# One PSUM tile per bank group in an attention-and-feed-forward kernel: three tiles in place of one of four banks

## The chip, the cores and the metric

The kernel runs on one core of a Trainium2 chip. The metric is the device time of one execution in microseconds (us), the median of three runs. Names of engines: PE is the TensorE matmul engine, ACT the ScalarE, DVE the VectorE, POOL the GpSimd, SP the queue that issues most transfers.

## What is computed

```python
def _attn_ref(q, k, v, agents):
    scale = 1.0 / np.sqrt(q.shape[-1])
    def sm(a, b):
        s = scale * (a @ b.transpose(0, 2, 1))
        s = s - s.max(-1, keepdims=True)
        e = np.exp(s)
        return e / (e.sum(-1, keepdims=True) + 1e-09)
    a2k = sm(agents, k)
    agent_v = a2k @ v
    q2a = sm(q, agents)
    return q2a @ agent_v
def _moe_ref(x, w_in, w_out):
    h = np.maximum(x @ w_in, 0.0)
    return h * h @ w_out
```

q, k and v are 4 x 12480 x 128, there are 49 agents per batch element, and the feed-forward part takes the 49920 rows of the attention's output through 2048 hidden channels (w_in 128 x 2048, w_out 2048 x 128).

## The kernel before

The agents' table is folded into the first feed-forward weight: `agent_v @ w_in` gives a table of 49 x 2048 per batch element, held as a high part (`aw_hi`) and a rest (`aw_ex`), so that the hidden layer comes straight from the query softmax, whose turned weights are `w` (98 rows and 30 copied rows) and `x` (the rest of the rows, copied to four row groups by transfers). Hidden channels are worked on in chunks of 128 for `G` = 480 tokens. Two groups of four chunks make a **session** (`m` == 2; four sessions at the start and two at the end have one group only, `m` == 1). There are 205 full sessions, and four of them make one block `g` of 960 tokens.

All eight PSUM banks belong to two sets of four banks, the tiles `A` and `B`. Sessions swap them. In a session whose first tile is, say, `A`:

- `first` (line 384) writes the first four chunks to the four banks of A: four matmuls of `w` with `aw_hi`, four of `x` with `aw_ex`. Then it does the same for the other four chunks in B.
- `rectified` (line 408) takes the ReLU out of PSUM into the SBUF tile `r` on ACT: for A first bank 0 alone, then banks 1 to 3; later B in one instruction of four banks.
- `second` (line 423) multiplies the squared hidden values of the session two before (`LAG` = 2) with `w_out`: 24 matmuls that all add up in `o`, which is **bank 0 of A**. The first four take `g_lo` of the first half, then sixteen alternate `wo_lo` and `wo_hi` with `g_hi`, and the last four take `g_lo` of the second half. After `LEAD` = 6 of them the phase "P" comes, in which PE does the side work, and then the other 18.
- The side work is the query softmax of a later block (`queries`, line 311) and the keys and values of the next batch element (`background`, line 448). It writes the other banks of A: bank 1 for query scores (`ASKED`), bank 2 for everything of `background` (`BLOCKS`), bank 3 for the turned query weights (`TURNED`).
- ACT then squares `r` in place (phase "A1" lies ahead of it, "A3" behind the session). DVE rounds the squares of the session before to `g_hi`, takes the rests `g_lo` in two halves with the side work of phase "D" between them, and at last adds `o` to `ob` in SBUF (`copied_out`, line 437). Every second session ends with a transfer of `ob` to HBM.

ACT, DVE and PE work through lists in the order in which the code issues them (`queued`, line 60, and `Ordered`, line 69, chain each instruction to the one before on its engine). Waits between engines are set by the framework from tiles: an instruction that writes a tile waits for those that read or wrote that tile before. The lines that matter for this:

```python
    ASKED, BLOCKS, TURNED = 1, 2, 3
    ...
        x = sets.tile([P, SET, 512], F32, name=tags[0])
        other = lambda: sets.tile([P, SET, 512], F32, name=tags[1])
    ...
        o = desk["at"][:, s % LAG if s < len(EARLY) else 0, :G]
    ...
            if m == 2:
                rectified(r, x, 0, 1)
                rectified(r, x, 1, 3)
```

Of the kernel before, what the change touches and what calls it, by code (L numbers as in the profile page):

```python
# [9 lines left out]
F32 = mybir.dt.float32  # L10
F32R = mybir.dt.float32r
U32 = mybir.dt.uint32
AF = mybir.ActivationFunctionType
# [4 lines left out]
P = 128  # L18
# [4 lines left out]
G = BLK // 2  # L23
SET = 4
EARLY = (1, 1, 1, 1)
SIZES = (2, 2)
LATE = (2, 1, 1)
LAG = 2
# [13 lines left out]
def agent_attention_relu2(ctx: ExitStack, tc: tile.TileContext, qT, kT, v, agT, w_in, w_out, outT):  # L42
    nc = tc.nc
    C, NTOK = qT.shape
    _, B, NA = agT.shape
# [14 lines left out]
    def queued(issue, eng, *args, **kw):  # L60

        with tc.issue_after(chain[eng]) if eng in chain else ExitStack():
            ins = issue(*args, **kw)  # L63
        chain[eng] = ins.ins
        return ins
# [3 lines left out]
    class Ordered:  # L69
        def __init__(self, eng, always=False):  # L70
            self.eng, self.always = eng, always
# [7 lines left out]
    pe, act, dve = (Ordered(e, True) for e in (nc.tensor, nc.scalar, nc.vector))  # L79
# [18 lines left out]
    ones = const.tile([P, P], F32, name="ones")  # L98
# [58 lines left out]
        pool.tensor_add(lo, t, rest)  # L157

    desk = {}
    ASKED, BLOCKS, TURNED = 1, 2, 3  # L160

    def bank():
        if alone[0]:
            return ps_h.tile([P, 2, 512], F32, name="h")[:, 0, :]
        return desk["at"][:, BLOCKS, :]

    def query_bank(slot):
        if alone[0]:
            return ps_a.tile([P, 512], F32, name="psa")
        return desk["at"][:, slot, :]  # L170

# [193 lines left out]
    def products(k, outs):  # L367
        g, j, at = place(k)
        b = g // NB
        w, x = weights[g][j]  # L370

        def main(n, **kw):
            cs = slice((at + n) * P, (at + n + 1) * P)
            queued(nc.tensor.matmul, nc.tensor, outs[n], state[b]["hi"][:, cs], w, **kw)

        def extra(n, **kw):
            t = (at + n) % NQ
            rows = slice(t * 32, t * 32 + NL)
            lo = state[b]["lo"][rows, (at + n) // NQ, :]
            queued(nc.tensor.matmul, nc.tensor, outs[n], lo, x[rows, :], **kw)  # L380

        return main, extra

    def first(k, m, x, other):
        outs = [x[:, n, :G] for n in range(SET)]
        main, extra = products(k, outs)
        for n in range(SET):
            main(n, start=True, stop=False)
        with tc.high_priority():
            for n in range(SET):  # L390
                extra(n, start=False, stop=True)
        if m == 2:
            y = other()
            outs += [y[:, n, :G] for n in range(SET)]
            with tc.high_priority():
                for n in range(SET, 2 * SET):
                    extra(n, start=True, stop=False)
            for n in range(SET, 2 * SET):
                main(n, start=False, stop=True)
            return x, y  # L400
        return x, None

    def held(name, dtype, m, at):
        if m == 2 or at == 0:
            tiles[name] = ffn.tile([P, 2 * SET, G], dtype, name=name, bufs=2)
        return tiles[name] if m == 2 else tiles[name][:, at : at + SET, :]

    def rectified(r, x, at, n):
        queued(nc.scalar.activation, nc.scalar, r[:, at : at + n, :], x[:, at % SET : at % SET + n, :G], AF.Relu)

    def squared(r, at, n):
        queued(nc.scalar.activation, nc.scalar, r[:, at : at + n, :], r[:, at : at + n, :], AF.Square)
# [35 lines left out]
    def background(b):  # L448
        kt = load_keys(b, 0, kv, "kt")
        for i in range(NK):  # L450
            yield "P", 1, True
            nxt = load_keys(b, i + 1, kv, "kt") if i + 1 < NK else load_values(b, 0, kv, "vt")
            yield from scores(b, i, kt)
            kt = nxt
        yield from maxima(b)
        vt = kt
        for i in range(NK):
            nxt = load_values(b, i + 1, kv, "vt") if i + 1 < NK else None
            yield from values(b, i, vt)
            vt = nxt  # L460
        yield from whole_sums(b)
        yield from tables(b)
# [3 lines left out]
    def step(gen):  # L466

        with ExitStack() as es:
            for ins in behind:
                es.enter_context(tc.issue_after(ins))  # L470
            return next(gen, None)
# [24 lines left out]

    def table(n, pieces=1):
        near = aw.tile([P, 512], F32R, name="aw_lo", bufs=3)
        pws = [bank() for _ in range(pieces)] if n < 2 else [desk["at"][:, n - 1, :]]
        w = 512 // pieces  # L500
        for x, pw in enumerate(pws):
            pe.matmul(pw[:, :w], turn["avT"], win[:, n * 512 + x * w : n * 512 + (x + 1) * w], start=True, stop=True)
        for x, pw in enumerate(pws):
            part = near[:, x * w : (x + 1) * w]
            act.activation(part, pw[:, :w], AF.Copy, scale=turn["signs"][:, :1])
            dve.scalar_tensor_tensor(
                out=hi[:, n * 512 + x * w : n * 512 + (x + 1) * w], in0=pw[:, :w], scalar=turn["signs"][:, 1:],
                in1=part.bitcast(F32), op0=ALU.mult, op1=ALU.subtract,
            )
# [13 lines left out]
    with tc.tile_pool(name="pre", bufs=PRE) as pre, tc.tile_pool(name="dec", bufs=2) as dec:  # L523
# [56 lines left out]
        for i in range(NK):  # L580
            _, rows, nt = blocks[i]
            n = rows * nt // 2
# [5 lines left out]
            s = sp.tile([P, 512], F32, name="s")[:, :n]  # L588
# [8 lines left out]
            if i in (0, 4, 8):  # L597
                at = i // 4 * WIDE
# [13 lines left out]
        f = small.tile([P, 1], F32, name="f")  # L612
# [88 lines left out]
    sets = ctx.enter_context(tc.tile_pool(name="sets", bufs=1, space=PSUM))  # L701
    ffn = ctx.enter_context(tc.tile_pool(name="ffn", bufs=4))

    sessions, starts, at = [], [], 0
# [47 lines left out]
    made, x, early = {}, None, None  # L752
    todo["end"] = starts[NB]
    for s in range(len(sessions) + LAG):
        k, m = sessions[s] if s < len(sessions) else (total, 0)
        if s == LAG:
            behind = [chain[eng] for eng in (nc.tensor, nc.sync, nc.scalar, nc.vector, nc.gpsimd)]
        if s in starts and s // 2 and starts.index(s) % NB == 0:
            assert not todo["next"]
            b = starts.index(s) // NB  # L760
            if b + 1 < B:
                todo.update(gen=background(b + 1), done=0, start=s, end=starts[(b + 1) * NB])
                todo["next"] = (*step(todo["gen"]), s)
        phase("L", s)

        tags = "AB" if s <= len(EARLY) or (s - len(EARLY)) % 2 == 0 else "BA"
        x = sets.tile([P, SET, 512], F32, name=tags[0])
        other = lambda: sets.tile([P, SET, 512], F32, name=tags[1])
        if s == 0:
            early = other()  # L770
        desk["at"] = early if s < len(EARLY) else x
        o = desk["at"][:, s % LAG if s < len(EARLY) else 0, :G]

        if m:
            x, y = first(k, m, x, other)
            r = held("r", F32, m, place(k)[2] % (2 * SET))
            made[s] = r
            if m == 2:
                rectified(r, x, 0, 1)
                rectified(r, x, 1, 3)  # L780
            else:
                for n in (0, 2):
                    rectified(r, x, n, 2)
        if s < LAG:
            alone[0] = True
            if s:
                for _ in range(5):
                    pe.matmul(desk["at"][:, 0, :P], ones, ones, start=True, stop=True)
            table(s + 2)
            alone[0] = False  # L790
        work = second(*sessions[s - LAG], o) if s >= LAG else iter(())
        for _ in range(LEAD):
            next(work, None)
        phase("P", s)
        if m == 2:
            rectified(r, y, SET, SET)
        phase("A1", s)
        if m == 2:
            squared(r, 0, 2 * SET)
        elif m:  # L800
            for n in (0, 2):
                squared(r, n, 2)
        if 1 <= s <= len(sessions):
            z, n = sessions[s - 1]
            old = made.pop(s - 1)
            hi = held("g_hi", F32R, n, place(z)[2] % (2 * SET))
            los = [ffn.tile([P, SET, G], F32R, name="g_lo", bufs=3) for _ in range(n)]
            parts[z] = hi, los
            if n == 2:
                rounded(hi, old, 0, 2 * SET)  # L810
                rest(los[0], old, hi, 0, SET)
                phase("D", s)
                rest(los[1], old, hi, SET, SET)
            else:
                for i in (0, 2):
                    rounded(hi, old, i, 2)
                    rest(los[0], old, hi, i, 2)
                phase("D", s)
        run(work)
        if s >= LAG:  # L820
            copied_out(*sessions[s - LAG], o)
        phase("A3", s)
# [35 lines left out]
```

## Time and profile before

| what | value |
|---|---|
| median of three runs | 2305.52 us (2304.36 to 2311.49) |
| profiled execution | 2305.71 us, its span 2303.9 us |
| mean granted TensorE clock | 0.987 of full speed |
| PE busy | 1954.8 us, 85% of the span |
| DVE busy | 1727.2 us, 75% |
| ACT busy | 1600.2 us, 69% |
| transfers | 57 GB/s mean, 17.1% of the 16 engines' time |

A timeline row gives the start in us, the length in us, the engine, the instruction as output<-inputs, how many rows of one kind it merges, and in brackets the idle time of the engine just before it with what ended that. Matmuls are pipelined: the next one starts before the printed length of the one before is over. All rows carry line 63, the helper that issues them, so the tile names tell the places apart. The first 84 us prepare the first batch element and the weights; the sessions run from there to about 2300 us.

### The profile page before, as it was taken

The numbers are of one execution on the slowest core, as the hardware profiler recorded it, in microseconds if no ns is written. First come the engines' busy times: TensorE is split into PE (matmuls) and PEld (weight loads), VectorE is DVE, ScalarE is ACT, GpSimd is POOL, SyncE is SP. The second block draws the span as 40 slices with busy tenths as digits, with TensorE's granted clock in tenths as the row PEclk, the third lists the DMA queues.
The fourth block names the chain that finished last, engine by engine and source line by source line (L and its number), as shares of the span: only waits on it lengthen the run. The fifth ranks groups of instructions, "written<-read, shape, count | busy, mean of one in ns | idle before, by whom it ended". The sixth has DMA issues, their size and how long they took to land.

```text
span 2303.9 us, 39309 instructions
## 1 busy us (share of the span) xinstructions
PE 1954.8 (85%) x17186; PEld 1466.7 (64%) x17186; DVE 1727.2 (75%) x1487; ACT 1600.2 (69%) x1213; POOL 20.8 (1%) x24
## 2 busy tenths in 40 slices
PE   8788888887888888888888888888888888888888
PEld 5566666665666666666666666666656666666666
DVE  7777777876777777787677777778777777777776
ACT  5766767766666767677576667777667777777775
POOL 3000000000000000000000000000000000000000
PEclk9999999999999999999899999999999999999999
DMA  9212112211112112111012210211111111101100
GB/s 335 80 57 75 53 47 75 65 54 42 34 63 69 56 49 70 63 60 60 30 34 73 68 48 30 78 59 56 43 31 33 41 33 41 33 32 36 32 24 20
DMA packets 54816, 131.44 MB, mean 57 GB/s; under 512 B 6508, under 2 KB 34828, under 8 KB 54644
## 3 DMA queue, kind: packets, MB, share of 16 engines
q1 hardware_dynamic: 54644, 128.93, 17.1%
q8 instruction: 135, 2.21, 0.4%
q14 instruction: 37, 0.30, 0.0%
HBM read 80.97 MB, written 25.56 MB: 46 GB/s over the span
## 4 chain that ended last, share of the span: by engine, by line
PE 72%; ACT 20%; DVE 6%; issue 2%; DVEq 0%; POOL 0%; ACTq 0%; POOLq 0%
PE A L63 36%; PE B L63 35%; ACT r L63 16%; ACT w L63 3%; DVE m L63 1%; ACT s L63 1%; DVE e L63 1%; DVE g_lo L63 1%; DVE g_hi L63 1%; DVE mx L63 0%; DVE t L63 0%; DVE aw_lo L63 0%; DVE av L63 0%; PE h L63 0%; ACT aw_hi L63 0%
## 5 line engine op out<-in xcount | busy, mean ns | idle before, releaser
L63 DVE TENSOR_TENSOR g_lo<-r,g_hi 128x1920 fp32r<-128x1920 f32 (+1 forms) x422 | 894.5, 2126 | 7.7 <-PE B L63 0.2
L63 ACT ACTIVATE r<-r 128x3840 f32<-128x3840 f32 (+1 forms) x217 | 712.1, 3285 | 2.2
L63 ACT ACTIVATE r<-B 128x1920 f32<-128x1920 f32 (+2 forms) x309 | 372.9, 1242 | 332.1 <-PE B L63 332.1
L63 ACT ACTIVATE r<-A 128x1920 f32<-128x1920 f32 (+3 forms) x318 | 380.1, 1232 | 225.4 <-PE A L63 225.4
L63 DVE CAST g_hi<-r 128x3840 fp32r<-128x3840 f32 (+1 forms) x217 | 448.4, 2066 | 0.1
L63 PE MATMUL A<-g_hi,wo_lo 128*128 128x480 f32 x832 | 333.3, 401 | 105.4 <-DVE e L63 44.0
L63 PE MATMUL B<-g_hi,wo_lo 128*128 128x480 f32 x832 | 331.3, 398 | 81.1 <-ACT w L63 46.0
L63 PE MATMUL A<-g_hi,wo_hi 128*128 128x480 f32 x832 | 324.7, 390 | 0.0
L63 PE MATMUL B<-g_hi,wo_hi 128*128 128x480 f32 x832 | 319.6, 384 | 0.0
L63 PE MATMUL A<-g_lo,wo_hi 128*128 128x480 f32 x832 | 228.0, 396 | 76.0 <-ACT r L63 76.0
L63 PE MATMUL B<-g_lo,wo_hi 128*128 128x480 f32 x832 | 227.8, 396 | 67.8 <-ACT r L63 67.8
L63 PEld LDWEIGHTS A<-g_hi,wo_lo 128*128 128x128 f32 x832 | 161.4, 194 | 147.7 <-issue 47.6
L63 PEld LDWEIGHTS A<-g_lo,wo_hi 128*128 128x128 f32 x832 | 149.8, 190 | 137.1 <-ACT r L63 117.6
L63 PEld LDWEIGHTS B<-g_hi,wo_lo 128*128 128x128 f32 x832 | 158.5, 191 | 121.1 <-ACT w L63 55.8
L63 PEld LDWEIGHTS B<-g_lo,wo_hi 128*128 128x128 f32 x832 | 149.6, 189 | 128.5 <-ACT r L63 109.1
L63 PE MATMUL A<-w,aw_hi 128*128 128x480 f32 x840 | 228.1, 393 | 2.6 <-DVE aw_hi L63 1.6
L63 DVE TENSOR_TENSOR ob<-B,ob 128x480 f32<-128x480 f32 x105 | 69.0, 657 | 211.6 <-PE B L63 211.6
L63 PE MATMUL B<-w,aw_hi 128*128 128x480 f32 x824 | 224.4, 394 | 0.0
L63 DVE COPY ob<-A 128x480 f32<-128x480 f32 x103 | 67.7, 657 | 196.7 <-PE A L63 190.7
L63 PEld LDWEIGHTS A<-w,aw_hi 128*128 128x128 f32 x840 | 150.0, 188 | 58.1 <-issue 34.2
L63 PEld LDWEIGHTS B<-w,aw_hi 128*128 128x128 f32 x824 | 147.3, 189 | 53.7 <-issue 34.4
L63 PEld LDWEIGHTS A<-g_hi,wo_hi 128*128 128x128 f32 x832 | 161.6, 194 | 24.3
(169 smaller groups left out, 1355.5 us busy)
## 6 DMA issues: line engine op xcount, KB each, us to landing
qt<-in_qT SPq DMA_DIRECT2D x52, 480.0 KB
out_T<-ob SPq DMA_DIRECT2D x104, 240.0 KB
kt<-in_kT SPq DMA_DIRECT2D x36, 512.0 KB
vt<-in_v SPq DMA_DIRECT2D x36, 512.0 KB
x<-w SPq DMA_DIRECT2D x416, 35.6 KB
ahead<-in_kT SPq DMA_DIRECT2D x12, 512.0 KB
ahead<-in_v SPq DMA_DIRECT2D x12, 512.0 KB
w<-w SPq DMA_DIRECT2D x104, 56.2 KB
```

The lines of the kernel that those rows point to most:

```text
L63: ins = issue(*args, **kw)
```

## The change

Each set of four banks becomes three tiles: one bank (`A0`), one bank (`A1`), and a pair (`A2`). `o` lies in the first, the work of `background` moves to the second (slot 1), and the query work keeps to the pair (slots 2 and 3). The ReLU takes one instruction per tile, so three of 480, 480 and 960 columns in place of two (480 and 1440) for the first half of a session and of one (1920) for the second half, and of two (960 each) in sessions of one group.

```diff
-    ASKED, BLOCKS, TURNED = 1, 2, 3
+    BLOCKS, ASKED, TURNED = 1, 2, 3
+    GROUPS = ((0, 1), (1, 1), (2, 2))
+
+    class Banks:
+        def __init__(self, tag):
+            self.tiles = [sets.tile([P, n, 512], F32, name=f"{tag}{at}") for at, n in GROUPS]
+
+        def __getitem__(self, n):
+            x = min(n, len(GROUPS) - 1)
+            return self.tiles[x][:, n - GROUPS[x][0], :]
...
-        return desk["at"][:, BLOCKS, :]
+        return desk["at"][BLOCKS]
...
-        return desk["at"][:, slot, :]
+        return desk["at"][slot]
...
-        outs = [x[:, n, :G] for n in range(SET)]
+        outs = [x[n][:, :G] for n in range(SET)]
...
-    def rectified(r, x, at, n):
-        queued(nc.scalar.activation, nc.scalar, r[:, at : at + n, :], x[:, at % SET : at % SET + n, :G], AF.Relu)
+    def rectified(r, x, at):
+        for bank, (n, m) in zip(x.tiles, GROUPS):
+            queued(nc.scalar.activation, nc.scalar, r[:, at + n : at + n + m, :], bank[:, :, :G], AF.Relu)
...
-        x = sets.tile([P, SET, 512], F32, name=tags[0])
-        other = lambda: sets.tile([P, SET, 512], F32, name=tags[1])
+        x = Banks(tags[0])
+        other = lambda: Banks(tags[1])
...
-        o = desk["at"][:, s % LAG if s < len(EARLY) else 0, :G]
+        o = desk["at"][s % LAG if s < len(EARLY) else 0][:, :G]
...
-            if m == 2:
-                rectified(r, x, 0, 1)
-                rectified(r, x, 1, 3)
-            else:
-                for n in (0, 2):
-                    rectified(r, x, n, 2)
+            rectified(r, x, 0)
...
-            rectified(r, y, SET, SET)
+            rectified(r, y, SET)
```

PE and DVE keep their instructions in the same order. What differs on PE is what its instructions wait for. The next two listings are one session with side work for a query block, on PE: from the second half of `first` (into A) over the start of `second` (`g_lo`, `g_hi` into B) to the turned query weights (`identr`) and what follows them. Before:

```order
L63 MATMUL A<-x_8966,aw_ex 128x480 x3
L63 MATMUL A<-w_8965,aw_hi 128x480 x4
L63 MATMUL B<-g_lo,wo_hi 128x480 [waits Activation_49]
L63 MATMUL B<-g_lo,wo_hi 128x480 x3
L63 MATMUL B<-g_hi,wo_lo 128x480
L63 MATMUL B<-g_hi,wo_hi 128x480
L63 MATMUL B<-identr,pp 98x120 x4
L63 MATMUL B<-g_hi,wo_lo 128x480 [waits Activation_49]
```

After, the same session, where the number behind a name is the tile's own (9941 is the bank with `o`, 9943 the pair of banks of the same set):

```order
L63 MATMUL A_9954<-x_9582,aw_ex 128x480 x2
L63 MATMUL A_9952<-w_9581,aw_hi 128x480
L63 MATMUL A_9953<-w_9581,aw_hi 128x480
L63 MATMUL A_9954<-w_9581,aw_hi 128x480 x2
L63 MATMUL B_9941<-g_lo,wo_hi 128x480 [waits Activation_49]
L63 MATMUL B_9941<-g_lo,wo_hi 128x480 x3
L63 MATMUL B_9941<-g_hi,wo_lo 128x480
L63 MATMUL B_9941<-g_hi,wo_hi 128x480
L63 MATMUL B_9943<-identr,pp 98x120 [waits Activation_49]
L63 MATMUL B_9943<-identr,pp 98x120 x3
L63 MATMUL B_9941<-g_hi,wo_lo 128x480
```

The wait on ACT behind the four `identr` matmuls is gone, and one ahead of them has come. The wait of the first `g_lo` stands, now for the tile of one bank.

On ACT the ReLUs of one session and the start of the next, with the ReLU of a first half at the top. Before:

```order
L63 ACTIVATE r<-A 128x480
L63 ACTIVATE r<-A 128x1440
L63 ACTIVATE r<-B 128x1920
L63 COPY s<-A 128x392
L63 ACTIVATE r<-r 128x3840
```

After:

```order
L63 ACTIVATE r<-A_11475 128x480
L63 ACTIVATE r<-A_11476 128x480
L63 ACTIVATE r<-A_11477 128x960
L63 ACTIVATE r<-B_11486 128x480
L63 ACTIVATE r<-B_11487 128x480
L63 ACTIVATE r<-B_11488 128x960
L63 COPY s<-A_11476 128x392
L63 ACTIVATE r<-r 128x3840
```

Three instructions have become six, with the same columns and the same neighbours.

On the SP queue some loads of keys and values stand behind the five small transfers of the query weights (`w`, `x`) that they stood ahead of. Before:

```order
L314 DMA qt<-in_qT 128x960
L180 DMA kt<-in_kT 128x1024 x2
L350 DMA w_1882<-w_1882 30x480
L352 DMA x_1883<-w_1882 19x480 x4
L446 DMA out_T<-ob 128x480
```

After:

```order
L323 DMA qt<-in_qT 128x960
L189 DMA kt<-in_kT 128x1024
L359 DMA w_1966<-w_1966 30x480
L361 DMA x_1967<-w_1966 19x480 x4
L189 DMA kt<-in_kT 128x1024
L456 DMA out_T<-ob 128x480
```

The second load of keys has moved behind `x`.

## Rows read from the trace of the kernel before

**Rows 1.** The page, part 1: busy us, share of the span, instructions of each engine.

```profile
PE 1954.8 (85%) x17186; PEld 1466.7 (64%) x17186; DVE 1727.2 (75%) x1487; ACT 1600.2 (69%) x1213; POOL 20.8 (1%) x24
```

**Rows 2.** Who waited for whom, PE: us in total, times, longest us.

```profile
PE A L63 <- ACT r L63: 77.0, 104, 1.9
PE B L63 <- ACT r L63: 68.5, 103, 1.9
PE B L63 <- ACT w L63: 46.0, 71, 0.7
...
PE A L63 <- DVE mb L63: 0.9, 2, 0.5
```

**Rows 3.** Groups of instructions by form: count, busy us, mean ns, idle before, releasers.

```profile
L63 PE MATMUL A<-g_hi,wo_lo 128*128 128x480 f32 x832 | 333.3, 401 | 105.4 <-DVE e L63 44.0 <-DVE av L63 28.4 <-DVE aw_lo L63 21.0
...
L63 PE MATMUL B<-g_hi,wo_lo 128*128 128x480 f32 x832 | 331.3, 398 | 81.1 <-ACT w L63 46.0 <-ACT s L63 14.4 <-DVE av L63 8.3
```

**Rows 4.** Timeline of PE, one session without side work and the next one's start.

```profile
590.22 1.03 PE L63 MATMUL A<-w,aw_hi 128*128 128x480 f32 x4
...
591.82 1.14 PE L63 MATMUL B<-w,aw_hi 128*128 128x480 f32 x4
593.68 1.13 PE L63 MATMUL A<-g_lo,wo_hi 128*128 128x480 f32 x4 [0.72 <-ACT r L63]
594.65 0.38 PE L63 MATMUL A<-g_hi,wo_lo 128*128 128x480 f32 x1
...
598.14 1.04 PE L63 MATMUL A<-g_lo,wo_hi 128*128 128x480 f32 x4
599.02 1.03 PE L63 MATMUL B<-w,aw_hi 128*128 128x480 f32 x4
...
600.30 0.39 PE L63 MATMUL A<-x,aw_ex 19*128 19x480 f32 x4
```

**Rows 5.** Timeline of PE around the turned query weights.

```profile
603.82 0.48 PE L63 MATMUL B<-identr,pp 120*98 120x120 f32 x4
604.95 0.49 PE L63 MATMUL B<-g_hi,wo_lo 128*128 128x480 f32 x1 [0.65 <-ACT w L63]
605.27 0.38 PE L63 MATMUL B<-g_hi,wo_hi 128*128 128x480 f32 x1
```

**Rows 6.** Timeline of PE around query scores.

```profile
613.96 0.89 PE L63 MATMUL A<-ag,qt 128*32 128x49 f32 x64
616.21 0.49 PE L63 MATMUL A<-g_hi,wo_lo 128*128 128x480 f32 x1 [1.36 <-DVE e L63]
```

**Rows 7.** Timeline of PE, query scores followed at once by other side work.

```profile
1003.48 0.89 PE L63 MATMUL A<-ag,qt 128*32 128x49 f32 x64
1004.20 0.89 PE L63 MATMUL A<-d,vt 128*32 128x49 f32 x64
```

**Rows 8.** Groups by form on ACT, the ReLUs.

```profile
L63 ACT ACTIVATE r<-B 128x1920 f32<-128x1920 f32 x103 | 183.7, 1784 | 0.0
...
L63 ACT ACTIVATE r<-A 128x1440 f32<-128x1440 f32 x103 | 140.8, 1367 | 0.0
...
L63 ACT ACTIVATE r<-A 128x480 f32<-128x480 f32 x103 | 59.1, 574 | 216.0 <-PE A L63 216.0
```

**Rows 9.** Timeline of ACT, the two ReLUs of a first half merged.

```profile
600.53 1.83 ACT L63 ACTIVATE r<-B 128x480 f32<-128x480 f32 x2 [1.78 <-PE B L63]
```

**Rows 10.** Timeline of DVE, the sum's copy at a session's end.

```profile
599.28 0.66 DVE L63 COPY ob<-A 128x480 f32<-128x480 f32 x1 [1.40 <-ACT r L63]
```

**Rows 11.** Stages: us; PE, PEld, DVE, ACT, POOL busy; PE clock, DMA share, GB/s.

```profile
84.00:2276.00 2192.00, 1866.99 (x16520) 1407.52 (x16519) 1651.88 (x1369) 1543.61 (x1114) 0.00 (x0) 0.99 0.16 50
...
399.36:410.44 11.08, 9.51 (x109) 7.36 (x108) 9.52 (x12) 8.21 (x7) 0.00 (x0) 1.00 0.18 56
...
1100.00:1170.00 70.00, 58.26 (x322) 42.64 (x321) 48.74 (x39) 45.05 (x33) 0.00 (x0) 0.93 0.10 31
```

**Rows 12.** Timeline of SP, two loads of keys merged.

```profile
177.30 12.37 SPq L180 DMA_DIRECT2D kt<-in_kT  x2
```

More of the change, by code (lines that the diff above doesn't have):

```diff
@@ L393, in first @@
             y = other()
-            outs += [y[:, n, :G] for n in range(SET)]
+            outs += [y[n][:, :G] for n in range(SET)]
             with tc.high_priority():
@@ L498, in table @@
         near = aw.tile([P, 512], F32R, name="aw_lo", bufs=3)
-        pws = [bank() for _ in range(pieces)] if n < 2 else [desk["at"][:, n - 1, :]]
+        pws = [bank() for _ in range(pieces)] if n < 2 else [desk["at"][4 - n]]
         w = 512 // pieces
@@ L787, in agent_attention_relu2 @@
                 for _ in range(5):
-                    pe.matmul(desk["at"][:, 0, :P], ones, ones, start=True, stop=True)
+                    pe.matmul(desk["at"][0][:, :P], ones, ones, start=True, stop=True)
             table(s + 2)
```

## The prediction

> **What bounds the kernel now.** I read the busy times first: PE is at 85%, DVE at 75%, ACT at 69% [rows 1]. PE is the fullest engine, yet it stands still for about 350 us of the span, so the next view is who it waits for. Two kinds of wait make up nearly all of it. The first matmul of `second` waits for ACT's ReLU in 207 sessions, 77.0 + 68.5 us [rows 2]. The first `g_hi` matmul behind side work waits for whoever reads that side work: DVE's `e`, `av` and `aw_lo`, ACT's `w` and `s`; its two groups sum to 105.4 + 81.1 = 186.5 us [rows 3], in about 184 waits, the first and the last kind of which stand in [rows 2] (46.0 us in 71 for `w`, 0.9 us in 2 for `mb`). In both kinds the matmul writes bank 0 (`o`), and the engine that it waits for is reading another bank of the same tile. For the first kind the timeline says so by length: in a session without side work the wait ends at 593.68 [rows 4], and the two merged ReLUs of a first half take 1.83 us [rows 9], of which the bank-0 one is 0.57 [rows 8]; PE waits for the second one too, which it does not need. So these waits come from where the tiles are cut, and the order of the work on PE would allow the next matmul.
>
> **Change, term 1: the ReLU wait.** A0 now holds `o` alone, and its ReLU lasts 0.57 us [rows 8] from when the first half's sums are in, while PE still has the second half's eight matmuls to issue (600.30 to some 601.5 in [rows 4]). So that ReLU ends before PE comes to `g_lo`, and I take the wait as gone. What a session gains is read as start to start, since a stopped pipeline drains and fills again: four matmuls in a row take 0.88 us (598.14 to 599.02), so `g_lo` could start at 591.82 + 0.88 = 592.70 and starts at 593.68, 0.98 later; and its own four then take 0.97 us (593.68 to 594.65) in place of 0.88 [rows 4]. That is 1.07 us a session, against 0.72 of printed idle. 207 x 1.07 = **221 us**.
>
> **Term 2: the side-work waits.** All 186.5 us of idle time [rows 3] go, because bank 1 and the pair are other tiles than `o`. The next write to them is the other half of the next session, many us later. Drain and fill add to it: behind `identr` PE restarts 1.13 us after its start, where the four need at most 0.48, so 0.65 plus a first matmul that takes 0.32 in place of 0.22, 0.75 in all for 0.65 of idle [rows 5]; behind query scores the gap is 2.25 us [rows 6], the same work followed at once by other work takes 0.72 [rows 7], so 1.53 for 1.36 of idle, plus 0.10. I take 0.18 over the idle time for each of 184: 33 us. Together **220 us**.
>
> **Term 3: the clock.** The granted clock of the sessions is 0.99 over 2192 us, and 0.93 in the stretch from 1100 to 1170 us, where PE waited longest behind side work [rows 11]; of the up to 22 us that this leaves, I take **15** back. The Trainium skill (TensorE: Matmul & The Clock Gate, A second HAM failure mode: psum-queue depth-cycling) says that small idle gaps between matmul groups, as PSUM banks are cycled, make the clock fall and return. By it all 22 us would come back, and the sum would be 7 us lower.
>
> **Term 4: more ReLUs.** 205 full sessions issue six in place of three, and six short ones three in place of two: 621 more ACT instructions. Column time is (1784 - 574) / 1440 = 0.84 ns, so 480 columns hold 0.17 us of fixed time [rows 8]; two back to back hide 0.11 of it (574 + 1367 against 1.83 [rows 9]). So one more costs 0.06 to 0.17 us, 37 to 106 us on ACT in all. I count nothing: ACT's 1543.6 us of the sessions' 2192 [rows 11] become at most 1650, below what is left of the span (2192 - 221 - 220 - 15 = 1736). Without that cover it costs up to 106 us. PE's new waits for the pair ahead of `identr` and query scores are for the third ReLU, 1.8 us behind the first half's sums; PE gets there after the second half and six matmuls, over 2.5 us behind them. Free, with nothing queued but PE itself.
>
> **Term 5: what is late next.** DVE has 1651.9 us in the sessions [rows 11], 7.98 for each of 207, against 1736 / 207 = 8.39 for PE. On average it keeps up, but not in each session: in the one from 399.36 to 410.44 DVE works 9.52 by the stage row, and some 9.7 with the gaps between its instructions, while PE's 9.51 loses 0.35 + 0.18 of drain and fill [rows 11], so PE would be through in 9.0. There `ob` comes late, and the next second half waits for it: in a plain session `ob` ends at 599.94 [rows 10] and A is written from 600.30 [rows 4], a cover of 0.36. I charge 0.7 us once in every four sessions, 52 x 0.7 = **36 us**, with neither the cover nor slack from other sessions set against it; both ends are 0 and twice this.
>
> **Term 6: SP's order.** Loads of keys that stood ahead of `w` and `x` now stand behind. Two such loads went out with 12.4 us from the first's start to the second's end [rows 12], each as soon as a buffer came free and one use ahead of the next; five small issues cannot make them late. Zero.
>
> **Sum.** 2305.7 (the profiled execution, span 2303.9 and 1.8 around it; the median of the runs is 0.2 lower) - 221 - 220 - 15 + 36 = 1885.7. I say **1886 us**, 18% less.
>
> **Rivals.**
> - *PE runs nearly through* (the forecast, 64%). 1835 (term 5 at nothing, all 22 us of clock, and 0.22 in place of 0.18 us over the idle time for each wait of term 2: 1886 - 36 - 7 - 7) to 1925 (term 5 doubled).
> - *DVE or ACT becomes the pace* (25%). After the change the three engines have 1736, 1652 and up to 1650 us of work, and DVE waits at `ob` for PE's last sum (0.26 us from 599.02 to 599.28 [rows 4, 10]). This decides if such hand-overs cost DVE over 8.39 - 7.98 = 0.41 us a session. At 1 us a session the sessions take 1652 + 207 = 1859 in place of 2192, and the time is 2305.7 - 333 = 1973. For it speaks how close the loads are; against it that DVE's wait for `ob` is 1.40 us now [rows 10] and `ob` is not what it works on next.
> - *Half of it* (6%). The ReLU wait goes, and a stall takes the place of the other, because the pair is written again while DVE still reads it or ACT's `w` comes later behind six ReLUs. 2305.7 - 221 = 2085. Against it: the next write to the pair lies most of a session off.
> - *Slower: reads and writes inside one set* (3%). ACT's ReLU of A1 and A2 now runs while PE writes A0, and DVE reads the pair likewise; before, PE wrote only the other set. If banks of one set got in each other's way and ReLUs took twice their 1.83 + 1.78 us [rows 8, 9], ACT's session would grow from at most 1650 / 207 = 7.97 to 11.6 against 10.6 of span now (2192 / 207): 207 x 1.0 = 207 us more, about 2510. It decides from 2.6 us a session, ReLUs at 1.7 times their length. Against it: ReLUs beside matmuls into the other set show the plain column time [rows 8]. The Trainium skill (PSUM — Partial Sum Buffer, PSUM bank collisions raise a hardware error) names the bank as what two engines must not share and reports accesses to different banks as clean; no row here has both in one set, and by it this rival would have no chance at all.
> - *It does not do what it says* (2%). PE still waits for the last ReLU of the set, and three ReLUs end up to 0.17 us later than two: 207 x 0.17 = 35, so 2341. The wait lists of the changed kernel, with a wait for the tile of `o` alone, speak against it.
>
> **How the numbers follow.** A measurement of this kernel can tell about 0.3% (7 us) from no change. Faster by more than that: the first three cases, 0.95. Slower: the last two, less what of the last would come out level, 0.04; no change 0.01. The range runs from 1835 to 1985: all of the forecast's own 1835 to 1925 (64%) and most of the second case, whose price is 1973 (20 of its 25%).
>
> **What would show it.** In the changed profile PE should have no wait for `r` of more than a few us in total, and none behind `identr`, `ag,qt`, `ag,kt` or `d,vt`; PE above 93% busy and the chain nearly all PE; DVE near 88 to 90%, its wait ahead of `ob` down to some tenths of a us; ACT near 87%; the first ReLU of each half at 0.57 us; a session without side work at about 7.75 us (8.80 before, 590.22 to 599.02 [rows 4]). Term 5 shows as waits of PE for `ob`, some 36 us. The forecast is wrong if PE waits for `ob` or `r` by over 90 us (second case), if `g_hi` still waits behind side work (third), or if a ReLU of 960 columns takes clearly more than 0.98 us, its columns by [rows 8] (fourth).

## The result, and the profile after

The changed kernel takes 1888.39 us (median; 1887.94 to 1890.64), the kernel before 2304.94 us on the same chip: a ratio of 0.819, 95% interval 0.8173 to 0.8206. The forecast was 1886 us, with a range of 1835 to 1985. The profiled execution took 1887.94 us, its span is 1885.8 us and the mean granted clock 0.997 (0.987 before).

The page's busy times answer to [rows 1]:

```profile
span 1885.8 us, 39996 instructions
PE 1859.1 (99%) x17186; PEld 1464.5 (78%) x17186; DVE 1715.7 (91%) x1487; ACT 1623.9 (86%) x1834; POOL 21.0 (1%) x24
```

PE's busy time fell too, by 95.7 us, though it runs the same 17186 instructions; its idle time fell from 349.1 to 26.7 us. The two together are the 418 us of span that went. ACT has 621 instructions more, as counted.

Who waited for whom on PE, us in total, times and longest, answers to [rows 2]. These are its rows of over half a us on the sessions' tiles A and B with a named engine:

```profile
PE B L63 <- DVE ob L63: 4.3, 8, 1.8
PE A L63 <- ACT r L63: 2.7, 4, 1.3
...
PE A L63 <- DVE ob L63: 1.6, 3, 0.5
PE A L63 <- DVE aw_hi L63: 1.6, 1, 1.6
PE B L63 <- ACT r L63: 1.4, 2, 0.7
...
PE B L63 <- DVE g_hi L63: 0.6, 1, 0.6
```

The 207 waits for the ReLU (145.5 us) are down to six, 4.1 us; those for `w`, `e`, `av`, `s` and `aw_lo` have no row in A or B any more. What came in their place is PE's wait for `ob`, 5.9 us. The page's chain that ended last, by engine, is now nearly all PE, with DVE next:

```profile
PE 90%; DVE 8%; ACT 1%; issue 1%; POOL 0%; DVEq 0%; ACTq 0%; POOLq 0%
```

PE's timeline in a session with both query scores and values, from the second half's `w` group to the second matmul behind the side work:

```profile
297.91 1.15 PE L63 MATMUL B<-w,aw_hi 128*128 128x480 f32 x4
298.89 1.03 PE L63 MATMUL A<-g_lo,wo_hi 128*128 128x480 f32 x4
299.76 0.38 PE L63 MATMUL A<-g_hi,wo_lo 128*128 128x480 f32 x1
299.98 0.37 PE L63 MATMUL A<-g_hi,wo_hi 128*128 128x480 f32 x1
300.28 0.89 PE L63 MATMUL A<-ag,qt 128*32 128x49 f32 x64
301.00 0.89 PE L63 MATMUL A<-d,vt 128*32 128x49 f32 x64
301.82 0.48 PE L63 MATMUL A<-g_hi,wo_lo 128*128 128x480 f32 x1
302.13 0.38 PE L63 MATMUL A<-g_hi,wo_hi 128*128 128x480 f32 x1
```

No row has an idle time in brackets. Against [rows 4], `g_lo` follows the `w` group after 0.98 us, where it took 1.86 (591.82 to 593.68); and `g_hi` follows the side work's last row after 0.82 us. ACT's timeline of the same session shows that the three ReLUs of a half, merged, take 1.90 us (1.83 before, [rows 9]):

```profile
297.79 1.90 ACT L63 ACTIVATE r<-A 128x480 f32<-128x480 f32 x3 [0.35 <-PE A L63]
299.55 1.92 ACT L63 ACTIVATE r<-B 128x480 f32<-128x480 f32 x3
301.50 3.42 ACT L63 ACTIVATE r<-r 128x3840 f32<-128x3840 f32 x1
```

### The profile page after: what moved, and what is told of

The parts are those of the page before. It is cut to its first block, busy times and chain, and to the rows that moved or that the text cites. A ratio compares the mean times of both kernels' runs of the same rounds, so it can differ in the third digit from the quotient of the medians.

```text
span 1885.8 us, 39996 instructions
## 1 busy us (share of the span) xinstructions
PE 1859.1 (99%) x17186; PEld 1464.5 (78%) x17186; DVE 1715.7 (91%) x1487; ACT 1623.9 (86%) x1834; POOL 21.0 (1%) x24
## 4 chain that ended last, share of the span: by engine, by line
PE 90%; DVE 8%; ACT 1%; issue 1%; POOL 0%; DVEq 0%; ACTq 0%; POOLq 0%
PE A L63 46%; PE B L63 42%; DVE g_lo L63 3%; DVE g_hi L63 2%; DVE ob L63 1%; DVE mx L63 1%; DVE z L63 1%; DVE e L63 1%; DVE t L63 0%; PE h L63 0%; ACT r L63 0%; DVE rest L63 0%; PE o L63 0%; PE psa L63 0%; DVE d L63 0%
## 5 line engine op out<-in xcount | busy, mean ns | idle before, releaser
L63 ACT ACTIVATE r<-r 128x3840 f32<-128x3840 f32 (+1 forms) x217 | 719.5, 3319 | 2.2
L63 ACT ACTIVATE r<-B 128x480 f32<-128x480 f32 (+1 forms) x618 | 393.3, 723 | 132.1 <-PE B L63 132.1
L63 ACT ACTIVATE r<-A 128x480 f32<-128x480 f32 (+1 forms) x630 | 400.8, 723 | 71.4 <-PE A L63 71.4
L63 PE MATMUL B<-g_hi,wo_lo 128*128 128x480 f32 x832 | 324.9, 390 | 1.3 <-ACT r L63 0.7
L63 PE MATMUL A<-g_hi,wo_hi 128*128 128x480 f32 x832 | 317.2, 381 | 0.0
L63 PE MATMUL A<-g_lo,wo_hi 128*128 128x480 f32 x832 | 215.1, 380 | 0.6 <-ACT r L63 0.6
L63 PE MATMUL B<-g_lo,wo_hi 128*128 128x480 f32 x832 | 214.9, 380 | 0.6 <-ACT r L63 0.6
L63 PEld LDWEIGHTS A<-g_lo,wo_hi 128*128 128x128 f32 x832 | 156.2, 188 | 25.9 <-ACT r L63 0.9
L63 PEld LDWEIGHTS B<-g_lo,wo_hi 128*128 128x128 f32 x832 | 156.2, 188 | 25.8 <-ACT r L63 0.9
L63 PEld LDWEIGHTS B<-g_hi,wo_hi 128*128 128x128 f32 x832 | 156.3, 188 | 23.4 <-issue 0.7
```

## The experiments

The theory: the time went because the sums `o` have a tile of their own, so that PE waits neither for the ReLUs of other banks nor for the readers of side work; PE's own work is now the bound, and ACT and DVE lie beside it. The rivals were that ACT or DVE has become the pace, that the second cut (blocks apart from query work) matters, and that splitting the ReLU alone does it. "Above" and "below" are against 1888.39 us by medians; the kernel before, run beside each group of experiments, stood between 2301.78 and 2304.94 us, so differences of some 3 us between groups mean nothing. All runs but one, the second below, came out within the range of their theory.

**The ReLU wait alone, put back.** Each half's ReLUs run in reverse order, so that the bank of the sums is cleared last:

```diff
-        for bank, (n, m) in zip(x.tiles, GROUPS):
+        for bank, (n, m) in list(zip(x.tiles, GROUPS))[::-1]:
```

> Changed kernel with the ReLUs of each half in reverse order, so that the bank of the sums is cleared last: this undoes the gain on the ReLU wait alone. Theory (that wait is worth 0.98 us a session, start to start): three ReLUs take 1.90 us in place of 0.58 for the first, PE stands still 0.7 to 0.8 us in 207 sessions with 0.1 to 0.2 for drain and fill, 2065 to 2100 us. Rival (DVE or ACT have become the pace, so PE has slack): the wait shows but costs less than half of it, 1930 to 1990 us.

Measured: 2093.09 us (ratio to the kernel before 0.9093, 0.9081 to 0.9106), 204.7 above. The waits on PE, and its timeline at one of them:

```profile
PE A L63 <- ACT r L63: 85.7, 105, 2.6
PE B L63 <- ACT r L63: 75.7, 103, 2.0
```

```profile
655.33 1.14 PE L63 MATMUL B<-w,aw_hi 128*128 128x480 f32 x4
657.26 1.14 PE L63 MATMUL A<-g_lo,wo_hi 128*128 128x480 f32 x4 [0.79 <-ACT r L63]
658.23 0.38 PE L63 MATMUL A<-g_hi,wo_lo 128*128 128x480 f32 x1
```

208 waits cost 204.7 us, 0.98 each, of which 0.78 is printed idle time. The wait costs its full price, so PE has no slack that would take it up, and the rival of a pace set by DVE or ACT falls here. Side work still stands apart in this kernel and has no waits.

**The side-work waits, put back.** Sums, blocks and query work share a tile of three banks, the fourth bank is alone. In one early session the query scores of one block overwrite the turned weights of another before ACT copies them (in the trace the scores are written at 87.81 us, the copy starts at 89.47), so what it computes from those weights is not valid. PE and DVE have as many instructions as in the changed kernel; ACT has four ReLUs a session in place of six.

```diff
-    BLOCKS, ASKED, TURNED = 1, 2, 3
-    GROUPS = ((0, 1), (1, 1), (2, 2))
+    BLOCKS, ASKED, TURNED = 1, 2, 2
+    GROUPS = ((0, 3), (3, 1))
...
-            x = min(n, len(GROUPS) - 1)
+            x = [at <= n < at + m for at, m in GROUPS].index(True)
```

> Changed kernel with all side work back in the tile of the sums: one tile of three banks (sums, blocks, and one bank for both kinds of query work), one tile of one bank. This undoes the gain on the side-work waits, and in part that on the ReLU wait, as the first ReLU is 1440 columns now. Theory: 186.5 us of idle plus 0.07 us for each of 184 waits come back, 199 us, and the ReLU of 1.4 us ends about 0.35 us after PE is ready, with 0.1 for drain and fill 0.45 x 207 = 93 us: 2120 to 2200 us. Rival (side-work waits cost only part of their idle time, since other work would have held PE anyway): 1990 to 2080 us.

Measured: 2218.97 us (0.9637, 0.9622 to 0.9651), 330.6 above and 19 over the theory's end. PE's waits, the largest rows, and its busy time:

```profile
PE 1956.0 (88%) x17186; PEld 1467.4 (66%) x17186; DVE 1725.7 (78%) x1487; ACT 1602.8 (72%) x1418; POOL 20.8 (1%) x24
```

```profile
PE B L63 <- ACT w L63: 51.8, 71, 0.7
PE A L63 <- DVE e L63: 44.0, 27, 2.4
PE A L63 <- DVE av L63: 30.1, 30, 1.5
PE A L63 <- ACT r L63: 25.8, 104, 1.5
PE A L63 <- DVE aw_lo L63: 21.0, 9, 2.7
PE B L63 <- ACT r L63: 20.3, 103, 1.5
PE B L63 <- ACT s L63: 14.4, 14, 1.1
```

The side-work waits are those of the kernel before, nearly to the count (71, 27, 30, 9, 14) and the us. The ReLU wait is smaller than I expected (46.1 us, not 0.35 x 207 = 72), and the total is larger, because PE's busy time came back as well: 96.9 us above the changed kernel's. So these waits cost more than their idle time, and more than the 0.07 us each over it that I had written there. The granted clock is 0.986, which is part of it: by the mean clocks some 25 of the 96.9 us.

**One kind of side work put back.** Blocks share a tile with the sums, query work stays apart:

```diff
-    GROUPS = ((0, 1), (1, 1), (2, 2))
+    GROUPS = ((0, 2), (2, 2))
...
-            x = min(n, len(GROUPS) - 1)
+            x = [at <= n < at + m for at, m in GROUPS].index(True)
```

> Changed kernel with the blocks' bank back in the tile of the sums, query work apart: two tiles of two banks. Theory: only the waits behind keys, values and tables come back (before: 90 us in about 82 waits named av, s, aw_lo, rl and mb, plus the share of sessions with both kinds, in which the other kind ended last, 5 to 35 us), and the first ReLU of 960 columns still ends in time: 1980 to 2020 us. Rival (the query work is what mattered, the blocks' readers are quick): under 1930 us.

Measured: 2004.76 us (0.8702, 0.8682 to 0.8722), 116.4 above. The four largest of PE's waits:

```profile
PE A L63 <- DVE av L63: 27.5, 30, 1.7
PE A L63 <- ACT s L63: 14.9, 25, 0.6
PE A L63 <- DVE aw_lo L63: 14.0, 9, 1.6
PE B L63 <- DVE av L63: 10.5, 9, 1.6
```

`w` and `e` have no row, and the ReLU of 960 columns is in time as well (3.0 us for `r` in A). So against the ReLU wait the sums need no bank of their own, only a first ReLU that ends before PE comes back; what costs here is the readers of side work in the same tile. That a tile shared without such a reader would be enough is argued from this; no run here has one.

**Is the second cut needed?** One bank for the sums, three banks in one tile for all side work:

```diff
-    GROUPS = ((0, 1), (1, 1), (2, 2))
+    GROUPS = ((0, 1), (1, 3))
```

> Two tiles per set in place of three: one bank for the sums, three banks for all side work, so four ReLU instructions a session in place of six. Theory (all that counts is that the sums have a tile of their own with a short ReLU; PE is the bound): no change from the changed kernel, 1882 to 1894 us, and again no waits of PE behind side work. Rival A (the second cut, blocks apart from query work, carries part of the gain): PE waits behind side work come back in the sessions that have both, 1910 to 1950 us. Rival B (ACT is close to being the pace): fewer ReLUs give 10 to 25 us, 1863 to 1878 us.

Measured: 1892.63 us (0.8222, 0.8209 to 0.8235), 4.2 above, and 2.1 above the run with eight ReLUs that shared its chip; its runs go from 1888.93 to 1895.11. By ratios it is 0.4% above the changed kernel, so a few us for the second cut are possible and 20 are not. PE's waits behind side work did not come back. What did come is DVE's `m` waiting for ACT's `s`, two uses of the tile that side work shares now; the kernel before had it too (25.8 us in 13). PE hardly feels it: its waits for `ob` are 6.6 us in all, against 5.9.

```profile
DVE m L63 <- ACT s L63: 14.9, 13, 3.8
```

```profile
PE B L63 <- DVE ob L63: 4.7, 8, 2.3
...
PE A L63 <- DVE ob L63: 1.9, 4, 0.5
```

With 416 fewer ACT instructions nothing was gained.

**The split without its cover.** The kernel before, its tiles whole, its ReLUs split into six:

```diff
-        queued(nc.scalar.activation, nc.scalar, r[:, at : at + n, :], x[:, at % SET : at % SET + n, :G], AF.Relu)
+        for c, d in ((0, 1), (1, 1), (2, 2)):
+            queued(nc.scalar.activation, nc.scalar, r[:, at + c : at + c + d, :], x[:, c : c + d, :G], AF.Relu)
...
-                rectified(r, x, 0, 1)
-                rectified(r, x, 1, 3)
+                rectified(r, x, 0, SET)
...
```

> Kernel before, with the ReLUs split as in the change (six a session) but the tiles left whole. This is the price of the split without its cover, since PE waits for the last ReLU. Theory: three ReLUs end 0.07 us later than two (1.90 against 1.83 us) in 207 sessions, 2312 to 2325 us. Rival 1 (each added instruction costs its fixed 0.17 us): 2335 to 2345 us. Rival 2 (waits are tracked by bank once each bank has its own ReLU, so that the split alone brings the gain): below 2150 us.

Measured: 2312.85 us against 2301.9 for the kernel before on that chip (1.0048, 1.0031 to 1.0066), 11 us slower. Two rows of PE's waits:

```profile
PE A L63 <- ACT r L63: 83.2, 104, 2.0
PE B L63 <- ACT r L63: 74.5, 103, 2.0
```

They are 12.2 us above [rows 2], 0.06 us a session. The split alone costs; the gain is in the tiles, since PE waits for the last ReLU of a whole tile although the bank that it needs has been cleared some 1.3 us before (the first of three ReLUs takes 0.58 of their 1.90 us).

**More ACT instructions under cover.** One ReLU per bank, eight a session:

```diff
-            queued(nc.scalar.activation, nc.scalar, r[:, at + n : at + n + m, :], bank[:, :, :G], AF.Relu)
+            for c in range(m):
+                queued(nc.scalar.activation, nc.scalar, r[:, at + n + c : at + n + c + 1, :], bank[:, c : c + 1, :G], AF.Relu)
```

> Changed kernel with one ReLU per bank, eight a session in place of six (412 more ACT instructions). Theory (PE is the bound, ACT's added time lies beside it): 1884 to 1894 us, ACT busy up by 25 to 70 us. Rival (ACT sets the pace in part): the time grows by most of what ACT grows, 1910 to 1950 us.

Measured: 1890.49 us (0.8211, 0.8199 to 0.8222), 2.1 above, no difference that can be told:

```profile
PE 1860.2 (98%) x17186; PEld 1465.5 (78%) x17186; DVE 1718.7 (91%) x1487; ACT 1649.6 (87%) x2250; POOL 20.6 (1%) x24
```

ACT took 25.7 us more for 416 instructions, 0.06 us each, and all of it was hidden.

**Less DVE work.** The query softmax is left unnormalised in the sessions:

```diff
-        dve.reduce_sum(z, e, axis=AX.X)
-        dve.tensor_scalar_add(z, z, 1e-9)
-        dve.reciprocal(z, z)
-        spare().tensor_mul(e, e, z.broadcast_to([TP, NT, NA]))
+        if alone[0]:
+            ...
```

> Changed kernel that leaves out, in the sessions, the normalisation of the query softmax: four DVE instructions, 1.5 us, in one of four sessions, the one in which DVE has most to do. Theory (PE is the bound, DVE's late sums are covered by slack; PE waits only 5.9 us for ob in all): 1880 to 1888 us. Rival (term 5 of the prediction: DVE is late once in four sessions and costs 0.7 us each time): 20 to 40 us less, 1848 to 1868 us.

Measured: 1880.89 us (0.8174, 0.8163 to 0.8185), 7.5 below by medians, 9.6 below the run with eight ReLUs on the same chip, 3.7 by ratios (0.0016 of 2302). Of 66.0 us that DVE no longer worked (1649.7 against 1715.7), at most 4 to 10 reached the end; the granted clock of this execution is 0.999 against 0.997, which alone could be some 4 us. PE's wait for `ob` fell to 2.9 us:

```profile
PE B L63 <- DVE ob L63: 1.9, 2, 1.0
...
PE A L63 <- DVE ob L63: 1.0, 3, 0.3
```

So DVE's late sums cost at most some 4 to 10 us in the changed kernel, not the 36 of term 5.

**The same on POOL.** To try this without leaving work out, the multiplication by 1/z went to POOL:

```diff
-        spare().tensor_mul(e, e, z.broadcast_to([TP, NT, NA]))
+        pool.tensor_mul(e, e, z.broadcast_to([TP, NT, NA]))
```

> Changed kernel with one DVE instruction of the query softmax (the multiplication of e by 1/z, 0.57 us in the session in which DVE has most to do) moved to POOL, which is idle in the sessions. Theory (PE is the bound and DVE's lateness costs it only a few us): 1882 to 1889 us, at most the 7.5 us below the changed kernel that leaving out the whole normalisation gave. Rival (POOL's work slows DVE beside it, or its longer instruction makes the query weights late): above 1895 us.

Measured: 1887.11 us (0.8192, 0.8177 to 0.8206), 1.3 below and within noise. POOL's row, busy us and mean ns behind the count:

```profile
L340 POOL TENSOR_TENSOR e<-e,z 120x392 f32<-120x392 f32 x51 | 95.2, 1867 | 1647.8 <-DVE z L63 1446.6 <-DVE d L63 104.8 <-ACT aw_hi L63 96.5
```

It takes 1.87 us there against 0.57 on DVE, off the path. DVE's busy time fell by 13.7 us (1702.0 against 1715.7), though 51 instructions of 0.57 us, 28.9 us, had left it: others of its instructions took longer, `d<-s,mb` above all (670 ns against 559). So that part of the rival is true, but it did not reach the end. It does not beat the changed kernel clearly, and no other version here does with the whole computation.

**More DVE work.** One difference of 480 columns more per full session, ahead of the copy of the sums:

```diff
                 rest(los[1], old, hi, SET, SET)
+                junk = ffn.tile([P, G], F32R, name="junk", bufs=1)
+                queued(nc.vector.tensor_sub, nc.vector, junk, old[:, 0, :], hi[:, 0, :].bitcast(F32))
```

> Changed kernel with one more DVE instruction of 480 columns (a difference that nothing reads) in each of the 205 full sessions, ahead of the copy of the sums: some 0.55 us more for DVE a session. It measures how far DVE is from setting the pace: the prediction put that at 0.41 us a session on average. Theory (the three engines share slack over several sessions, so that only what exceeds that average shows): 205 x (0.55 - 0.41) = 29 us and some more in the sessions with most DVE work, 1905 to 1960 us. Rival A (slack is ample): 1886 to 1895 us. Rival B (DVE already sets the pace in the changed kernel): 205 x 0.55 = 113 us more, 1990 to 2010 us.

Measured: 1920.08 us (0.8333, 0.8316 to 0.8351), 31.7 above:

```profile
PE 1873.6 (98%) x17186; PEld 1468.3 (77%) x17186; DVE 1827.6 (95%) x1692; ACT 1626.2 (85%) x1834; POOL 21.0 (1%) x24
```

```profile
PE 66%; DVE 30%; issue 2%; ACT 1%; POOL 0%; DVEq 0%; ACTq 0%; POOLq 0%
```

```profile
PE B L63 <- DVE ob L63: 20.3, 44, 2.4
```

DVE worked 111.9 us more, 0.55 a session, and 80 of that was hidden: 0.39 us a session. That this is near the prediction's 0.41 is partly luck. The 0.41 was a mean over sessions forecast at 1736 us in all; from 84 to 1862 us the changed kernel's take 1778 us and DVE works 1639 of them, so the mean slack is 0.67 us a session, of which this work could use 0.39. Beyond that, DVE's share of the chain goes from 8 to 30%, and PE's waits for `ob` from 4.3 to 20.3 us in B. The second rival is thus a true limit; for work added to every session it lies some 0.4 us a session away.

## Why the prediction was right

The mechanism held: both kinds of wait went, each for the reason given, and nothing of their size took their place. The sum came within 3 us, but four of its terms were off: the waits were priced too high, the clock too low, and late sums were charged that hardly came. That the errors cancelled is luck. The parts of it, in us:

| part | forecast | measured |
|---|---|---|
| idle time of PE in both kinds of wait | 332 | 322, all of PE's idle time, new waits set against it |
| drain and fill around them (terms 1 and 2) | 109 | 71 |
| clock (term 3) | 15 | 24 |
| DVE's late sums (term 5) | -36 | -4 to -10, already in the rows above |
| sum | 420 | 418 of span |

Measured drain and fill is worked out: 95.7 us less busy time, less the clock's part, 2303.9 x 0.013 - 1885.8 x 0.003 = 24; so 71 us for 391 waits, 0.18 each. The reverse-order run tells the two kinds apart: it has 53.1 us more busy time than the changed kernel, about 3 of them clock, for 202 more waits, so 0.25 for a wait for the ReLU; that leaves about 0.1 for one behind side work. The forecast had 0.35 and 0.18.

- **Term 1** (forecast 221 us). The reverse-order run prices at 204.7 us a wait that is a little longer than the one removed, since three ReLUs stand ahead of it in place of two; the split-only run puts that at 11 us, so some 194 us are left for this term. The step that failed is the 0.88 us for the `w` group ahead of `g_lo`, taken from a group that follows like work. In the changed kernel that group takes 0.98 us (297.91 to 298.89) without a wait: it follows the matmuls of 19 rows, and 0.10 us of what I booked as drain is the switch between the two, 21 us in all.
- **Term 2** (220 us). What the two kinds lost together leaves 418 + 7 (the late sums) - 194 - 24 = 207 us for it. The failing step is the first matmul behind side work, whose 0.32 in place of 0.22 I laid to the wait: without one it takes 0.31 (301.82 to 302.13), so it belongs to the change of shape; over 184 waits that is 18 us too much.
- **Term 3** (15 us of at most 22). 24 us came back, counting the stretches ahead of and behind the sessions. The Trainium skill's rule (TensorE: Matmul & The Clock Gate, A second HAM failure mode: psum-queue depth-cycling), by which all of it should return once the small gaps are gone, agrees with the 0.997 here. But the reverse-order run has 208 gaps of 0.78 us and a granted clock of 0.996, and the run with side work beside the sums has 0.986, so here the clock went with the waits behind side work. The kernel before shows which of them: from 84 us on its granted clock is at the lower level (1.2 GHz) in 13 stretches of 3 to 7 us, and each begins in the last us of a wait of PE of 1.9 us or more, or within 1.4 us after. Eleven of these waits are for `e` or `aw_lo`, two for the ReLU of the last, short sessions. Ten other waits as long have no such stretch behind them, and none of the usual waits of 0.7 us has one. One of the 13, with PE's wait, then the clock (0.51, the third number from the right):

```profile
525.90 0.46 PE L63 MATMUL A<-g_hi,wo_lo 128*128 128x480 f32 x1 [2.72 <-DVE aw_lo L63]
```

```profile
526.50:529.50 3.00, 3.00 (x10) 2.46 (x9) 1.32 (x1) 1.12 (x2) 0.00 (x0) 0.51 0.14 34
```

- **Term 4** (nothing). Right. Of the 37 to 106 us that it put on ACT, the split-only run shows 38.1 (1638.3 against 1600.2 busy, 0.06 us an instruction) and the changed kernel 23.7 (1623.9), under the range; where the cover is gone, 11 us reach the time.
- **Term 5** (36 us). Off by a factor of four or more. Here is a session of the changed kernel with the same side work, one block earlier than the one that the prediction read: the stage row, and DVE's `ob` rows on either side:

```profile
306.05:315.55 9.50, 9.50 (x111) 7.68 (x110) 9.36 (x12) 8.22 (x10) 0.00 (x0) 1.00 0.05 13
```

```profile
306.05 0.66 DVE L63 COPY ob<-A 128x480 f32<-128x480 f32 x1 [0.34 <-PE A L63]
...
315.55 0.65 DVE L63 TENSOR_TENSOR ob<-B,ob 128x480 f32<-128x480 f32 x1
```

DVE does set its length (no idle time ahead of the second `ob`). But PE's session is 9.21 us long (305.85 to 315.06), not 9.0, and `ob` starts 0.49 us behind PE's last group in place of 0.20. That 0.29 us fits into the cover of 0.36 which the prediction named and then set at nothing. The next session has less for DVE to do, and the lag is gone (`ob` at 324.17 waits for PE again, by 0.57 us). The session that the prediction read, here from 341.93 to 351.42, shows the same: 9.49 us, and `ob` 0.52 us behind PE.
- **Term 6** (nothing): PE waited for no load of keys or values in the sessions.

Of the rivals, *half of it* and *slower* fell. The ReLU that runs beside matmuls into its own set is the pair's of a first half: above, the three ReLUs end at 299.69 and PE writes A again from 298.89. In the groups by form the ReLU of 960 columns, first and second halves together, takes 1001 ns:

```profile
L63 ACT ACTIVATE r<-A 128x960 f32<-128x960 f32 x210 | 210.2, 1001 | 0.0
```

In the split-only run, where PE waits until the last ReLU of a first half has ended, it takes 996 ns, so the matmuls beside it cost it nothing that can be told. The Trainium skill (PSUM — Partial Sum Buffer, PSUM bank collisions raise a hardware error) reports accesses to different banks as clean; these durations agree.

*It does not do what it says* is what the split-only run shows in isolation: 11 us, where 35 was the bound. Of the things to look for, DVE came to 91%, a little over the 88 to 90 forecast, ACT to 86% (87), and a session without side work in PE's timeline to 7.82 us (526.15 to 533.97; 7.75).

## What to carry to other kernels

Where an engine waits for a reader of another bank, as here, look at the cut of the tiles before the order of the work: give the buffer that the busiest engine comes back to first a tile of its own, and clear it first. Splitting the instructions without splitting the tile only cost time here. Price a removed stop by the start-to-start time that the same sequence has elsewhere without one, since the switch between unlike matmuls looks like refill; and before charging an engine's lateness, set it against the cover that the trace shows.

## What was not expected of the hardware

- A stop of PE costs about 0.18 us beyond its printed idle time (71 us over 391 waits; 0.25 for the ReLU's, about 0.1 behind side work), so busy time falls when waits go: 95.7 us here, clock included.
- One more ReLU in a row costs ACT 0.06 us (25.7 us for 416), though 480 columns alone show 0.17 us of fixed time [rows 8].
- 208 gaps of 0.78 us left the granted clock at 0.996; with the waits behind side work, up to 2.7 us long, it was 0.986 and 0.987. In the kernel before each fall came at or just behind a wait of 1.9 us or more, but not each such wait has one; what decides between them stays open.
